# A routed two-expert layer behind linear attention: first visits of the last two routing units dispatched ahead of second ones, a third buffer of loaded rows, and one load issued two blocks earlier

## The chip, the cores and the metric

The kernel runs on one core of a Trainium2 chip. The metric is device time in microseconds (us), the median of several runs. A profiled execution gives the trace. The engines are PE (TensorE matmuls, with its weight loads PEld), DVE (VectorE), ACT (ScalarE), POOL (GpSimd) and SP (SyncE). Here POOL issues the weight loads and all indirect transfers, SP issues the other loads and stores of the routed part; all of them run on the core's 16 DMA engines.

## The reference, cut to what matters

Linear attention makes 4608 token rows of 512 values. A noisy gate picks two of eight experts for each token; each expert is a two-layer net, 512 to 1024 to 512. A token's output is the sum of its two experts' results, weighted.

```python
x = attn_out.transpose(0, 2, 1, 3).reshape(4608, 512)
logits = x @ w_gate
noisy_logits = logits + np.log1p(np.exp(x @ w_noise)) * noise
top2 = np.argpartition(-noisy_logits, 2, axis=1)[:, :2]
top2_w = softmax(noisy_logits at top2)
for e in range(8):
    for k in range(2):
        mask = top2[:, k] == e
        h = np.maximum(x[mask] @ w1[e], 0.0)
        out[mask] += top2_w[mask, k, None] * (h @ w2[e])
```

## The kernel before

**Lists.** Of a token's two experts, the one with the lower number is its first visit (kind `F`), the other its second visit (kind `S`). There are 16 lists in DRAM (`x_sorted`): one of first and one of second visits for each expert. A first visit writes its weighted result to `part`; the second visit gathers that row again (tile `L`), adds its own result and scatters the sum to the output. Tiles of kind `M` take the ends of an expert's two lists together, and their rows come by gather (tile `xm`).

**Routing.** Tokens are routed in five units (`UNITS`): units 0 to 2 have nine groups of 128 tokens each, unit 3 has six, unit 4 three. `rt_a`, `rt_b`, `rt_c` work out each token's place in its two lists (tile `posi`, written in `rt_c`). `dispatch` then sends every group twice with an indirect DMA on POOL, once for each visit (`sl` 0 and 1), and a short memset behind each keeps the issues apart. Tables of bounds (`ROUNDS`) let early loads read the front of some lists before later units have been sent; `early` declares which transfers don't touch each other's rows. Every load that has no such declaration waits until the dispatches ahead of it in the program have landed.

**Blocks.** The experts' work goes by blocks of up to 4 tiles of 128 rows. `x_load` loads a block's rows on SP: either turned by the DMA (tile `xt`), or as they are (`turned=False`, tile `xn`, from the pool `pb.np`) with the transposes done on PE in `xn_t`. `mm1` and `mm2` are the two layers, `put` stores first visits to `part` on SP and scatters second visits on POOL.

**Order.** The program is written out by hand and engines take their instructions in that order. `interval(cur, prev, weights, nxt)` interleaves three blocks on PE: the first layer of `cur`, the second layer of `prev` with its puts, and the transposes of `nxt`. The function `routing` covers the stretch that is changed; its blocks are, in order of use:

- `a0` (expert 0) and `a1` (expert 1, 3 tiles of first visits), `a2` (expert 2, 2 tiles): loaded during attention
- `b0`, `b1`, `b2` (experts 0, 1, 2; 2 tiles each) and `a3` (expert 3, 3 tiles): loaded after unit 2, by the bounds
- `c0` (expert 0, tiles 6 to 9 of first visits, 448 rows): the first block that needs its list complete, so it waits for all dispatches that can write to it

After `routing` comes a loop over `c0` and 19 more blocks. The first of the 19 (called block 1 here) is expert 1's tiles 5 and 6 of first visits; its `xn`, and the meta values of expert 1's second visits (`meta1S`), are loaded on SP behind `c0`'s load and the puts of `b2`.

In the trace the lines to know are L398 (dispatch), L442 (weights: `w1` and `w2` of an expert, 1 MB each as stored), L504 (gather of `xm`), L449 (meta loads), L571 and L574 (loads of `xn`: whole tiles, and the last half tile), L594 (PE transposes of `xn`), L647 (`mm1`), L662 (`mm2`), L630 (gather of `L`), L678 (store to `part`).

Of the kernel before, what the change touches and what calls it, by code (L numbers as in the profile page):

```python
# [7 lines left out]
FP32 = mybir.dt.float32  # L8
BF16 = mybir.dt.bfloat16
INT32 = mybir.dt.int32  # L10
# [5 lines left out]
P = 128  # L16
B, H, S, D = 8, 8, 576, 64
N_TOK = B * S
HD = H * D
E = 8  # L20
F = 1024
# [17 lines left out]
ROW_W = 576  # L39
# [81 lines left out]
class PhaseA:  # L121
# [266 lines left out]

        self.nc.gpsimd.memset(self.c["gap"], 0.0)  # L389

    def dispatch(self, u, a=0, z=9):

        tc = self.tc
        g, c0, c1 = UNITS[u]
        for ci in range(c0 + a, min(c1, c0 + z)):
            for sl in range(2):
                self.nc.gpsimd.nop()
                r = self.nc.gpsimd.indirect_dma_start(  # L398
                    out=self.x_sorted,
                    out_offset=bass.IndirectOffsetOnAxis(ap=self.r["posi", u][:, ci - c0, sl : sl + 1], axis=0),  # L400
                    in_=self.xr[g % 2][:, ci, :].bitcast(INT32), in_offset=None,
                )
                tc.declare_no_dep(r.ins, group="disp", reason="every (token, expert) pair has its own row")
                for i, (after, q) in enumerate(ROUNDS):
                    if after < u:
                        tc.declare_no_dep(r.ins, group=f"read{i}", reason="that round reads rows below its bound")
                        tc.add_to_no_dep_group(f"past{i}", r.ins)
                tc.add_to_no_dep_group("disp", r.ins)
                self.apart()


class PhaseB:
# [31 lines left out]
    def meta_load(self, e, kind, i0, nt, group=None):  # L444

        m = self.mp.tile([P, nt, 4], INT32, name=f"meta{nt}{kind}" if group is None else f"early{e}_{i0}")
        row = self.row(e, kind, i0)
        rows = self.x_sorted[row : row + nt * P, HD // 2 : HD // 2 + 4]
        r = self.nc.sync.dma_start(out=m[:], in_=rows.rearrange("(t p) c -> p t c", p=P))  # L449
        self.early(r, group)  # L450
        for i in range(nt):
            self.m[e, kind, i0 + i] = {"gate": m[:, i, 1 : 2] if kind == "F" else m[:, i, 2 : 3]}
        if kind == "S":
            self.raw[e] = m
# [90 lines left out]
        m = [P // 2 if half(*t) else P for t in tiles]  # L545
        return {"e": e, "parts": parts, "tiles": tiles, "m": m, "n": sum(m), "nt": len(m), "L": {}}

    def early(self, r, i):

        if i is not None:  # L550
            self.tc.declare_no_dep(r.ins, group=f"past{i}", reason="that round reads rows below its bound")
            self.tc.add_to_no_dep_group(f"read{i}", r.ins)

    def x_load(self, b, group=None, turned=True):


        nc, e, t = self.nc, b["e"], 0
# [5 lines left out]
        for kind, i0, n in b["parts"]:  # L563
            if kind != "M":
                row, m = self.row(e, kind, i0), sum(b["m"][t : t + n])
                src = lambda a, z: self.x_sorted[row + a : row + z, 0 : HD // 2].bitcast(BF16)
                k = m // P
                if turned:
                    r = nc.sync.dma_start(out=b["xt"][:, :, t * P : t * P + m], in_=src(0, m), transpose=True)
                else:  # L570
                    r = nc.sync.dma_start(out=b["xn"][:, t : t + k], in_=src(0, k * P).rearrange("(t p) d -> p t d", p=P))  # L571
                self.early(r, group)
                if k < n and not turned:
                    nc.sync.dma_start(out=b["xn"][0 : P // 2, t + k], in_=src(k * P, m))  # L574
            t += n

    def xn(self, b, t, dc):
# [140 lines left out]
    def general(self):  # L718

        nc, tc, c = self.nc, self.tc, self.c  # L720
# [12 lines left out]
        with tc.If(total > 0):  # L733
            for l in range(2 * E):
                e, kind = l % E, "FS"[l // E]
# [4 lines left out]
                rows = nc.values_load(ovi[0:1, l : l + 1], min_val=0, max_val=N_TOK + P)  # L740
                with tc.For_i(0, rows - (P - 1), P) as i:
                    b = self.block(e, (kind, 0, 1))
                    xn = self.mp.tile([P, ROW_W // 2], INT32, name="xn", bufs=1)
                    nc.sync.dma_start(out=xn[:], in_=self.x_sorted[bass.ds(i + l * REGION, P)])
                    tp = self.ps_y[0].tile([P, 1024], BF16, name="b")
                    for dc in range(4):
# [6 lines left out]
                    if kind == "S":  # L753
# [4 lines left out]
                        nc.vector.scalar_tensor_tensor(out=gi[:], in0=meta[:, 3:4], scalar=float(NO_P), in1=inv[:],  # L758
                                                       op0=ALU.min, op1=ALU.max)
                        nc.vector.tensor_scalar_add(out=end[:], in0=end[:], scalar1=-float(P))  # L760
                        L = b["L"][0] = self.mp.tile([P, HD], FP32, name="L", bufs=1)
                        nc.gpsimd.nop()
                        nc.gpsimd.indirect_dma_start(
                            out=L[:].bitcast(INT32), out_offset=None, in_=self.part.bitcast(INT32),
# [145 lines left out]
def routing(pa, pb, c, a0, a1, a2):  # L910
# [3 lines left out]
    a3, c0 = pb.block(3, ("F", 0, 3)), pb.block(0, ("F", 6, 4))  # L914
# [11 lines left out]
    pa.rt_c(3)  # L926
    pb.mm2(a0, 0)
    pb.put(a0, 0)
    pa.dispatch(3, 0, 3)
    pb.w_load(3, 0)  # L930
    pa.dispatch(3, 3, 6)
    pb.mm2(a0, 1)
    pb.put(a0, 1)
    pa.rt_a(4)
# [1 line left out]
    pa.rt_b(4)  # L936
    pb.mm1(a1, 6, 7)
    pa.rt_c(4)
    pa.dispatch(4)
    pb.w_load(3, 1)  # L940
    pb.mids()
    pb.meta_load(2, "F", 2, 2, 2)
    pb.x_load(b2, 2, False)
# [1 line left out]
    pb.x_load(a3, 2, False)  # L945
    pb.interval(a2, a1, (), b0)
    pb.interval(b0, a2, (), b1)
    pb.interval(b1, b0, (), b2)
    pb.interval(b2, b1, (), a3)
    pb.prepare(0)  # L950
    pb.x_load(c0, turned=False)
    pb.interval(a3, b2, (), c0)
    return a3, c0

# [19 lines left out]
def kernel(  # L974
# [24 lines left out]
    with ExitStack() as order:  # L999
        order.enter_context(tc.manual_schedule())  # L1000
        right = lambda name, bufs: ctx.enter_context(tc.tile_pool(name=name, bufs=bufs, side="right"))
        with ExitStack() as rout:
# [11 lines left out]
            pb.ps_h = [ps(ctx, "ps_h2", 3, "right")]  # L1014
            pb.ps_t = ps(ctx, "ps_t", 1, "right")
            pb.xps += [pb.xp] * 3 + [right("B_x2", 1)]
            pb.np = right("B_n", 2)
            pb.lp = right("B_l", 8)
            pb.yp += [right("B_y2", 6)] * 2
            pb.wp.append(right("B_w2", 3))  # L1020
            prev, cur = routing(pa, pb, c, *first)
        pb.ps_y.append(ps(ctx, "ps_y2", 2, "left"))
        pb.wp.append(ctx.enter_context(tc.tile_pool(name="B_w3", bufs=1, side="left")))
        blocks = [cur] + [pb.block(e, *parts) for e in range(1, E) for parts in PLAN[e]]

        todo = {}
# [55 lines left out]
```

## Time and profile before

| | us |
|---|---|
| time, median of 3 runs | 435.69 (435.42 to 435.72) |
| profiled execution, span from first to last instruction | 439.8 |
| PE matmuls busy | 353.5 (80%) |
| POOL busy | 280.4 (64%) |
| DVE busy | 185.5 (42%) |
| ACT busy | 172.9 (39%) |
| PE idle just before the transposes of `c0` | 6.4 |

The busy shares are means over the whole span: attention, with PE about half busy, takes up to some 140 us, the routed layer the rest. What a change to one stretch is worth is to be read in that stretch, from the waits and the order of the queues there. A trace time counts from the start of the span; a row of the timeline gives start, duration, engine, line, operation, tiles, count, and in brackets how long the engine was idle before it and what ended that.

### The profile page before, as it was taken

What the parts mean: (1) busy time and instruction counts of PE and PEld (TensorE: products, weight loads), DVE (VectorE), ACT (ScalarE), POOL (GpSimd) and SP (SyncE); (2) the same over time, 40 slices, a digit from 0 to 9 for tenths busy, and PEclk for the clock granted to TensorE, in tenths of its full rate; (3) what the DMA queues carried; (4) which work ended last, traced back from release to release, by engine and by line L of the source; (5) the groups of instructions that cost most, each with busy time, mean ns of one, the idle gap of its engine ahead of it and who ended that gap; (6) DMA issues with size and microseconds to landing.
All of it is one profiled execution on the core that took longest, in us unless ns stands there. A gap on an engine that the chain in (4) does not pass through costs nothing.

```text
span 439.8 us, 6877 instructions
## 1 busy us (share of the span) xinstructions
PE 353.5 (80%) x2497; PEld 211.7 (48%) x2497; DVE 185.5 (42%) x474; ACT 172.9 (39%) x310; POOL 280.4 (64%) x408
## 2 busy tenths in 40 slices
PE   3494576365745889994999999989999999999990
PEld 1293465254522456662555655644554554554440
DVE  2745989997543773120124204213331331231240
ACT  1709545760620243441444543344334334334310
POOL 7120228888888878761001848348988879778892
PEclk9858756768895699997899999999999999999996
DMA  9999997499989899999953999999988759644441
GB/s 130 206 208 207 230 213 174 107 224 236 186 192 212 165 223 213 376 211 239 233 137 109 198 211 247 215 236 194 257 177 200 212 141 232 184 150 144 154 149 51
DMA packets 83186, 85.58 MB, mean 195 GB/s; under 512 B 42656, under 2 KB 65891, under 8 KB 83143
## 3 DMA queue, kind: packets, MB, share of 16 engines
q0 software_dynamic: 36160, 63.91, 66.1%
q1 hardware_dynamic: 45318, 20.96, 21.7%
q10 hardware_dynamic: 1664, 0.18, 0.5%
q8 instruction: 21, 0.34, 0.3%
q14 instruction: 23, 0.18, 0.1%
HBM read 77.13 MB, written 33.79 MB: 252 GB/s over the span
## 4 chain that ended last, share of the span: by engine, by line
PE 45%; DMA 16%; POOL 15%; DVE 9%; issue 8%; another core or an unknown queue 2%; ACT 2%; POOLq 0%; SPq 0%; DVEq 0%; ACTq 0%
PE b L647 20%; PE b L662 20%; POOL x_sorted L398 5%; DMA v<-in_v_dram 4%; DMA w<-in_moe_w_dram 3%; DMA xn<-x_sorted 3%; POOL out_dram L684 3%; POOL L L630 3%; DMA meta5S<-x_sorted 2%; DVE xr L283 2%; DMA x_sorted<-xr,posi 1%; PE misc L209 1%; POOL gap L692 1%; DMA L<-part,gi 1%
## 5 line engine op out<-in xcount | busy, mean ns | idle before, releaser
L649 ACT ACTIVATE hT<-b 128x256 bf16<-128x256 f32 (+5 forms) x224 | 101.3, 461 | 158.0 <-PE b L647 141.4
L647 PE MATMUL b<-xt,w 128*128 128x256 bf16 (+5 forms) x896 | 153.7, 320 | 9.9 <-DMA xt<-x_sorted 4.2
L662 PE MATMUL b<-w,hT 128*128 128x512 bf16 (+1 forms) x640 | 145.8, 383 | 2.2 <-DVE y L666 2.2
L647 PEld LDWEIGHTS <-w 128*128 128x128 bf16 x896 | 88.2, 101 | 67.9 <-issue 16.2
L398 POOL DMA_INDIRECT x_sorted<-xr,posi x72 | 76.5, 1063 | 23.8 <-issue 12.2
L662 PEld LDWEIGHTS <-hT 128*128 128x128 bf16 (+1 forms) x640 | 59.3, 99 | 65.8 <-issue 6.2
L630 POOL DMA_INDIRECT L<-part,mgi x12 | 12.1, 1006 | 61.1 <-DMA part<-y 41.5
L178 ACT ACTIVATE e<-kq 128x2304 bf16<-128x2304 bf16 x16 | 33.3, 2127 | 24.4 <-DMA kq<-in_k_dram 9.4
L684 POOL DMA_INDIRECT out_dram<-y,si x34 | 33.7, 992 | 9.2 <-issue 5.1
L630 POOL DMA_INDIRECT L<-part,gi x34 | 34.9, 1027 | 6.9 <-issue 5.4
L209 PEld LDWEIGHTS <-e 64*128 64x128 bf16 x288 | 22.1, 126 | 20.0 <-DVE e L190 14.4
L272 PE MATMUL num<-kvbd,pqt 128*64 128x162 bf16 x288 | 16.8, 281 | 16.5 <-issue 9.3
L668 DVE TENSOR_SCALAR y<-b,early 128x512 f32<-128x512 f32 x18 | 13.4, 750 | 37.9 <-PE b L662 28.7
L209 PE MATMUL b<-v,e 64*128 64x192 bf16 x144 | 21.0, 320 | 10.4 <-DVE e L190 7.0
L209 PE MATMUL misc<-v,e 64*128 64x192 bf16 x144 | 20.9, 319 | 6.4 <-DMA v<-in_v_dram 6.0
L272 PEld LDWEIGHTS <-pqt 128*64 128x64 bf16 x288 | 14.0, 136 | 19.1 <-issue 10.5
L283 DVE TENSOR_TENSOR xr<-num,rden 128x768 bf16<-128x768 f32 x24 | 21.9, 952 | 0.4
L190 DVE TENSOR_TENSOR e<-e,kq 128x2304 bf16<-128x2304 bf16 x16 | 21.4, 1356 | 0.3
L637 POOL MEMSET gap<- 128x416 f32 x46 | 21.2, 462 | 0.1
L692 POOL MEMSET gap<- 128x416 f32 x45 | 20.9, 465 | 0.0
L389 POOL MEMSET gap<- 128x192 f32 x72 | 19.9, 276 | 0.0
L666 DVE SCALAR_TENSOR_TENSOR y<-b,mgate,L 128x512 f32<-128x512 f32 (+1 forms) x12 | 8.9, 746 | 25.9 <-PE b L662 10.1
(170 smaller groups left out, 314.3 us busy)
## 6 DMA issues: line engine op xcount, KB each, us to landing
w<-in_moe_w_dram POOLq DMA_DIRECT2D x16, 1024.0 KB
part<-y SPq DMA_DIRECT2D x39, 256.0 KB
kq<-in_k_dram POOLq DMA_DIRECT2D x8, 576.0 KB
kq<-in_q_dram POOLq DMA_DIRECT2D x8, 576.0 KB
v<-in_v_dram POOLq DMA_DIRECT2D x8, 576.0 KB
x_sorted<-xr,posi POOLq DMA_INDIRECT x72
xn<-x_sorted SPq DMA_DIRECT2D x4, 256.0 KB
part<-y SPq DMA_DIRECT2D x7, 128.0 KB
```

What stands on the lines that cost most here:

```text
L178: self.nc.scalar.activation(out=e, in_=x, func=ACT.Exp)
L190: nc.vector.tensor_tensor(out=e, in0=e, in1=x, op=ALU.min)
L209: nc.tensor.matmul(out=self.kvps[g, h, j][:, KVM * i : KVM * i + KVM], lhsT=e[half, hp, ci, :], rhs=v[half, hp::4, 64 * ci : 64 * ci + 64] ...
L272: nc.tensor.matmul(out=ps[half, hp, KVW * i : KVW * i + KVW], lhsT=self.pqt[g, 3 * t + i][:, hp, half], rhs=self.kvbd[g][:, j, hp, :], sta ...
L283: nc.vector.tensor_tensor(out=_ap(xr, [[64, 4], [ROW_W, 3], [1, 64]], off=3 * t * ROW_W + 256 * s), in0=_ap(ps, [[512, 4], [KVW, 3], [1, 6 ...
L398: r = self.nc.gpsimd.indirect_dma_start(out=self.x_sorted, out_offset=bass.IndirectOffsetOnAxis(ap=self.r["posi", u][:, ci - c0, sl : sl + ...
L630: r = nc.gpsimd.indirect_dma_start(out=L[0:m].bitcast(INT32), out_offset=None, in_=self.part.bitcast(INT32), in_offset=bass.IndirectOffset ...
L647: nc.tensor.matmul(out=ps[:, 0:n], lhsT=w1[:, dc, fc * P : fc * P + P], rhs=b["xt"][:, dc, 0:n], start=(dc == 0), stop=(dc == 3))
L649: nc.scalar.activation(out=b["hT"][:, fc, 0:n], in_=ps[:, 0:n], func=ACT.Relu)
L662: nc.tensor.matmul(out=ps[i * m : i * m + m], lhsT=b["hT"][:, f, t * P : t * P + m], rhs=w2[:, f, :], start=(fc == 0), stop=(fc == 8 // n ...
L684: r = nc.gpsimd.indirect_dma_start(out=self.out, out_offset=bass.IndirectOffsetOnAxis(ap=self.m[e, kind, i]["si"][0:m], axis=0), in_=y[0:m ...
L692: nc.gpsimd.memset(self.c["gap2"][:], 0.0)
```

## The change

Four things are done, all in or for the function `routing`:

- `dispatch` takes a list of visits. Unit 3 sends its six first visits, unit 4 its three, and only then do the second visits of both follow. The load of expert 3's second weight (`w_load(3, 1)`) now stands between the first and the second visits; it stood behind all dispatches.
- `early` declares that lists of first visits hold no second visits. A load from a list of first visits no longer waits for second visits, and a dispatch of second visits no longer waits for such loads. The half-tile load in `x_load` gets the same declaration.
- the pool of `xn` has three buffers, not two. To make room, two tiles of the fallback `general`, which handles overfull lists, move to a pool of their own.
- `prepare(0)` (a meta load) and `x_load(c0)` stand ahead of the intervals of `b1` and `b2`; they stood behind them.

```diff
-    def dispatch(self, u, a=0, z=9):
+    def dispatch(self, u, a=0, z=9, visits=(0, 1)):
...
-            for sl in range(2):
+            for sl in visits:
...
+                if sl:
+                    tc.declare_no_dep(r.ins, group="first", reason="lists of first visits hold no second visits")
+                    tc.add_to_no_dep_group("second", r.ins)
...
-    def early(self, r, i):
-
+    def early(self, r, kind, i):
+
+        if kind == "F":
+            self.tc.declare_no_dep(r.ins, group="second", reason="lists of first visits hold no second visits")
+            self.tc.add_to_no_dep_group("first", r.ins)
...
-                    nc.sync.dma_start(out=b["xn"][0 : P // 2, t + k], in_=src(k * P, m))
+                    r = nc.sync.dma_start(out=b["xn"][0 : P // 2, t + k], in_=src(k * P, m))
+                    self.early(r, kind, group)
...
-    pa.dispatch(3, 0, 3)
+    pa.dispatch(3, 0, 6, (0,))
     pb.w_load(3, 0)
-    pa.dispatch(3, 3, 6)
...
-    pa.dispatch(4)
+    pa.dispatch(4, visits=(0,))
     pb.w_load(3, 1)
+    pa.dispatch(3, 0, 6, (1,))
+    pa.dispatch(4, visits=(1,))
...
     pb.interval(b0, a2, (), b1)
+    pb.prepare(0)
+    pb.x_load(c0, turned=False)
     pb.interval(b1, b0, (), b2)
     pb.interval(b2, b1, (), a3)
-    pb.prepare(0)
-    pb.x_load(c0, turned=False)
     pb.interval(a3, b2, (), c0)
...
-            pb.np = right("B_n", 2)
+            pb.np = right("B_n", 3)
```

On POOL, from the load of expert 3's first weight to the first gather of `xm`, the order before is this (dispatches and their memsets repeat: six with `posi_1912`, unit 3, then six with `posi_2084`, unit 4):

```order
L442 DMA w1_1851<-in_moe_w1_dram 128x4x1024
L398 DMA x_sorted<-xr1_184,posi_1912 73984x288
...
L398 DMA x_sorted<-xr1_184,posi_2084 73984x288
...
L442 DMA w2_1852<-in_moe_w2_dram 128x8x512
L504 DMA xm_2598<-x_sorted,m_idx_2118 128x288
```

After the change three dispatches of unit 4 (`posi_2066`) come first, then the second weight, then nine dispatches of second visits (six with `posi_1912`, unit 3, and three with `posi_2066`, unit 4):

```order
L445 DMA w1_1851<-in_moe_w1_dram 128x4x1024
L398 DMA x_sorted<-xr1_184,posi_2066 73984x288
...
L445 DMA w2_1852<-in_moe_w2_dram 128x8x512
L398 DMA x_sorted<-xr1_184,posi_1912 73984x288
...
L398 DMA x_sorted<-xr1_184,posi_2066 73984x288
...
L507 DMA xm_2601<-x_sorted,m_idx_2118 128x288
```

The second weight has moved from behind twelve dispatches to behind three; the gather of `xm` still stands behind all of them.

On SP, from the last puts of `a2` (the first row) to the load of block 1 (the last row), the order before is this; the six puts between are those of `b0`, `b1` and `b2`, two each:

```order
L678 DMA part<-y_2274 128x512
L678 DMA part<-y_2323 128x512
L678 DMA part<-y_2347 128x512
L678 DMA part<-y_2407 128x512
L678 DMA part<-y_2431 128x512
L449 DMA meta4F_2475<-x_sorted 128x4x4
L571 DMA xn_2477<-x_sorted 128x3x512
L574 DMA xn_2477<-x_sorted 64x512
L678 DMA part<-y_2502 128x512
...
L449 DMA meta1S_2586<-x_sorted 128x4
L571 DMA xn_2588<-x_sorted 128x2x512
```

After the change:

```order
L685 DMA part<-y_2274 128x512
L452 DMA meta4F_2301<-x_sorted 128x4x4
L577 DMA xn_2303<-x_sorted 128x3x512
L580 DMA xn_2303<-x_sorted 64x512
L685 DMA part<-y_2328 128x512
...
L452 DMA meta1S_2589<-x_sorted 128x4
L577 DMA xn_2591<-x_sorted 128x2x512
```

The three loads for `c0` now stand ahead of the puts of `b0` and `b1`; the load of block 1 still stands behind the puts of `b2` and behind `meta1S`.

## Rows read from the trace of the kernel before

**Rows 1.** The page's part 1: busy us, share of the span, instructions.

```profile
PE 353.5 (80%) x2497; PEld 211.7 (48%) x2497; DVE 185.5 (42%) x474; ACT 172.9 (39%) x310; POOL 280.4 (64%) x408
```

**Rows 2.** Waits of PE, 140 to 440 us: who, for what: total, times, longest.

```profile
PE t L594 <- DMA xn<-x_sorted: 6.4, 1, 6.4
...
PE b L662 <- DVE y L666: 2.2, 1, 2.2
```

**Rows 3.** Timeline of PE, 184 to 300 us.

```profile
191.08 0.61 PE L594 MATMUL t<-ident,xn 128*128 128x128 bf16 x8
191.52 1.04 PE L647 MATMUL b<-xt,w 128*128 128x256 bf16 x8
...
196.91 1.46 PE L647 MATMUL b<-xt,w 128*128 128x384 bf16 x8
198.21 1.89 PE L662 MATMUL b<-w,hT 128*128 128x512 bf16 x8
206.50 1.04 PE L594 MATMUL t<-ident,xn 128*128 128x128 bf16 x8 [6.40 <-DMA xn<-x_sorted]
...
214.45 1.89 PE L662 MATMUL b<-w,hT 128*128 128x512 bf16 x8
...
219.41 0.61 PE L594 MATMUL t<-ident,xn 128*128 128x128 bf16 x8
...
295.94 1.89 PE L662 MATMUL b<-w,hT 128*128 128x512 bf16 x8 [2.16 <-DVE y L666]
```

**Rows 4.** Stretches: us, busy by engine, granted PE clock, DMA share, GB/s.

```profile
206.00:208.00 2.00, 1.50 (x11) 1.17 (x12) 0.00 (x0) 0.43 (x1) 0.00 (x0) 0.50 1.33 230
...
214.00:216.00 2.00, 2.00 (x12) 0.92 (x10) 0.00 (x0) 1.04 (x2) 0.00 (x0) 1.00 1.11 231
```

**Rows 5.** The chain that ended last, 140 to 210 us: start, us, what.

```profile
193.65 12.81 DMA xn<-x_sorted
```

**Rows 6.** Timeline of SP's queue, 100 to 302 us (the first: 178 to 181).

```profile
177.36 1.45 SPq L678 DMA_DIRECT2D part<-y  x2
...
193.65 0.82 SPq L571 DMA_DIRECT2D xn<-x_sorted  x1
...
201.80 0.48 SPq L449 DMA_DIRECT2D meta1S<-x_sorted  x1
202.38 8.83 SPq L571 DMA_DIRECT2D xn<-x_sorted  x2
...
270.28 13.57 SPq L569 DMA_TRANSPOSE xt<-x_sorted  x1
283.95 1.11 SPq L678 DMA_DIRECT2D part<-y  x2
```

**Rows 7.** Timeline of POOL, 140 to 262 us, its memsets left out.

```profile
166.23 0.82 POOL L442 DMA_DIRECT2D w<-in_moe_w_dram  x1
...
178.66 0.97 POOL L398 DMA_INDIRECT x_sorted<-xr,posi  x1 [1.58 <-DMA w<-in_moe_w_dram]
...
184.29 0.97 POOL L398 DMA_INDIRECT x_sorted<-xr,posi  x1 [0.17 <-issue]
...
189.91 1.07 POOL L504 DMA_INDIRECT xm<-x_sorted,m_idx  x1 [3.50 <-DVE y L668]
...
193.02 1.79 POOL L442 DMA_DIRECT2D w<-in_moe_w_dram  x2
```

**Rows 8.** Timeline of DVE, 150 to 240 us.

```profile
161.52 0.26 DVE L376 CAST posi<-rank 128x6 int32<-128x6 f32 x1
...
212.61 0.16 DVE L465 TENSOR_TENSOR si<-meta1S,inv 128x1 int32<-128x1 int32 x1 [11.60 <-DMA meta1S<-x_sorted]
```

**Rows 9.** Stretches of 10 us, columns as in Rows 4.

```profile
190.00:200.00 10.00, 9.77 (x66) 5.75 (x64) 1.50 (x2) 4.70 (x10) 9.36 (x12) 1.00 1.13 228
...
220.00:230.00 10.00, 10.00 (x61) 5.56 (x59) 1.87 (x3) 4.57 (x9) 0.00 (x0) 1.00 0.56 148
...
290.00:300.00 10.00, 7.84 (x40) 3.41 (x39) 3.00 (x5) 2.95 (x6) 7.81 (x11) 1.00 0.80 230
```

**Rows 10.** The last stretch, columns as in Rows 4.

```profile
396.00:440.00 44.00, 32.03 (x172) 15.69 (x170) 9.00 (x12) 10.89 (x22) 31.68 (x43) 0.90 0.38 125
```

**Rows 11.** Timeline of POOL, 345 to 400 us.

```profile
396.28 1.05 POOL L630 DMA_INDIRECT L<-part,gi  x1 [1.55 <-DMA part<-y]
```

More of the change, by code (lines that the diff above doesn't have):

```diff
@@ L449, in meta_load @@
         r = self.nc.sync.dma_start(out=m[:], in_=rows.rearrange("(t p) c -> p t c", p=P))
-        self.early(r, group)
+        self.early(r, kind, group)
         for i in range(nt):
@@ L571, in x_load @@
                     r = nc.sync.dma_start(out=b["xn"][:, t : t + k], in_=src(0, k * P).rearrange("(t p) d -> p t d", p=P))
-                self.early(r, group)
+                self.early(r, kind, group)
                 if k < n and not turned:
-                    nc.sync.dma_start(out=b["xn"][0 : P // 2, t + k], in_=src(k * P, m))
+                    r = nc.sync.dma_start(out=b["xn"][0 : P // 2, t + k], in_=src(k * P, m))
+                    self.early(r, kind, group)
             t += n
@@ L742, in general @@
                     b = self.block(e, (kind, 0, 1))
-                    xn = self.mp.tile([P, ROW_W // 2], INT32, name="xn", bufs=1)
+                    xn = self.late.tile([P, ROW_W // 2], INT32, name="xn", bufs=1)
                     nc.sync.dma_start(out=xn[:], in_=self.x_sorted[bass.ds(i + l * REGION, P)])
@@ L760, in general @@
                         nc.vector.tensor_scalar_add(out=end[:], in0=end[:], scalar1=-float(P))
-                        L = b["L"][0] = self.mp.tile([P, HD], FP32, name="L", bufs=1)
+                        L = b["L"][0] = self.late.tile([P, HD], FP32, name="L", bufs=1)
                         nc.gpsimd.nop()
@@ L1023 @@
         pb.wp.append(ctx.enter_context(tc.tile_pool(name="B_w3", bufs=1, side="left")))
+        pb.late = ctx.enter_context(tc.tile_pool(name="B_late", bufs=1, side="left"))
         blocks = [cur] + [pb.block(e, *parts) for e in range(1, E) for parts in PLAN[e]]
```

## The prediction, made before the changed kernel ran

> **What bounds the kernel now.** I read the busy times first: PE is the busiest engine, 353.5 of 439.8 us [rows 1]. So what counts behind the attention part is PE's own waits. From 140 us to the end PE waits for a transfer once: 6.4 us in its transposes (L594) for a load of `xn`; the next one is 2.2 us for DVE, at 294 us [rows 2]. PE's timeline places the first: PE has ended its work at 200.10 and stands until 206.50 [rows 3]. The chain of waits names the load: issued on SP at 193.65, landed 12.81 later, at 206.46 [rows 5]; by the order on SP this is the load of `c0`. The idle stretch has a second price. In the stretch 206 to 208 us the granted clock is 0.50, that is 1.2 of 2.4 GHz, and at 214 to 216 us it is 1.00 again [rows 4]; ahead of the wait it was 1.00 [rows 9]. Between the two, PE works at half speed.
>
> From there to the end PE stands close to its work: its only larger gap is the 2.16 us at 294 us [rows 3]. The last stretch belongs to POOL, which gathers and scatters expert 7's tiles one behind the other from 396.28 on (31.68 us busy in the stretch, PE 32.03) [rows 10]; but that row of tiles starts when a store to `part` has landed [rows 11], a store of a result of PE. So a time that PE gains at 200 us is passed on to the end unless something between is bound by transfers.
>
> **The change part by part.**
>
> *The load of `c0` moves up.* Now it stands on SP behind the puts of `b1`, and reaches the queue at 193.65 [rows 6]. After the change it stands behind the last put of `a2`. SP ends that put at 178.81 [rows 6]. The load then needs the nine first visits of units 3 and 4. Unit 4's places are worked out at 161.8 [rows 8], so its first visits can be sent right behind the weight load of 166.23, in the places that unit 3's dispatches had. POOL has eight transfers in flight: the one at 178.66 stood 1.58 us for the weight load eight places before it, so this one landed at about 178.5 [rows 7], and I take the three dispatches behind it to land by 180. So `c0`'s load is issued at about 181, not 193.65. With the duration it had, 12.81 [rows 5], it lands at about 194, six us ahead of 200.10. It lands no sooner than the dispatches, so 181 is the floor; the ceiling is the first rival. The wait of 6.40 us goes.
>
> *The half clock goes with it.* From 206.50 to 214.45 PE ran 8 transposes, 8 matmuls of 384 columns, 8 transposes and 16 matmuls of 384 columns [rows 3]: 7.95 us. At full clock 8 transposes took 0.44 (191.08 to 191.52) and 8 such matmuls 1.30 (196.91 to 198.21) [rows 3]. Full speed makes 0.44 + 1.30 + 0.44 + 2.60 = 4.78. Saved: 3.17 us. Together 6.40 + 3.17 = **9.57 us**.
>
> *What is late next.* Block 1's transposes stand at 219.41 now, without a wait [rows 3]; with 9.57 less they stand at 209.84. Its load doesn't move: it is issued at 202.38, behind `meta1S` and the puts of `b2`, which still follow PE [rows 6]. Its 256 KB may take 12.81 x 256/448 = 7.3 us if the duration goes by size (landed at 209.7, no wait), or 12.81 if it goes by what else is under way (215.2, wait 5.35). `meta1S`, issued at 201.80, landed by 212.61, 10.8 us later, with `c0`'s load ahead of it [rows 6, 8]; without that it will be quicker. I take the middle of the two bounds, 10.0 us: landed at 212.4, a wait of **2.5 us**, since the two weight loads issued at 193.02 [rows 7] will be under way then as they were beside `c0`'s load. Such a wait keeps the clock: after the 2.16 us at 294 us it is 1.00 over the whole stretch [rows 3, 9].
>
> Here a page speaks for less. The Trainium skill ("DMA: Bandwidth & Descriptors", section on the anatomy of one DMA) fits a DMA from GpSimd with 2.0 us plus bytes over 436 GB/s, which would be 2.9 us for the 384 KB of `c0`'s larger load and, an estimate by that page, 2.6 us for block 1's; then the wait of 2.5 falls away and the sum is 430.2. The trace disagrees for a queue under load: 12.81 us.
>
> *The third buffer.* With two, SP stood inside the two loads issued from 202.38 for 8.83 us [rows 6], until `c0`'s transposes had freed a buffer. With three it goes on at once. Nothing that PE waits for stands behind it there, so I cost it at nothing; without it `c0`'s early load would have to wait for the transposes of `b2`, which is why it belongs to the first item.
>
> *First visits first, and the weight between.* The number of dispatches, memsets and weight loads on POOL is the same. What moves is the weight's 1 MB: from behind the last dispatch to ahead of nine. Its first use is the second layer of `a3`, now at 214.45 [rows 3], then about 205; it is earlier in both. The second visits land later by what the weight takes, at most 166.23 to 178.5, 12.3 us [rows 7], and by what `c0`'s load takes of the DMA engines. Who waits: the gather of `xm` at 189.91 [rows 7], all of POOL behind it (four weight loads for experts 4 and 5) and `meta1S` on SP. PE needs `xm` only for the block behind block 1 and the weights far behind, and the DMA engines, full at 190 to 200 us (share 1.13), are half idle at 220 to 230 (0.56) [rows 9]; so this is covered as long as the second visits have landed when SP comes to `meta1S` at 201.80. I expect them at 195 to 199: 189.91 and 5 to 9 us. The puts of `b0` and `b1` come behind `c0`'s load on SP; their results wait in buffers and nobody on PE waits for the stores.
>
> *Behind 220 us.* The 2.16 us at 294 us come from a gather that waited for a store, which stood on SP behind a load (270.28, 13.57 us) [rows 6] that waits for PE to free its buffer. That goes with PE, so I leave it as it is.
>
> The sum against the profiled span: 439.8 - 9.57 + 2.5 = 432.7. The median of the runs stands to that span as 435.69 to 439.8, 0.9907: **428.7 us**.
>
> **The rivals.**
>
> 1. *`c0` is late still.* Its load meets the weight that was moved up. If the weight's 12.3 us come wholly ahead of it, it lands at 181 + 12.3 + 12.81 = 206.1, and all but 0.4 us stays: 435.3. If half of it, at 200.0, and nothing stays. Against it: the two are in different queues and the load's own 12.81 was measured beside two weight loads. 0.05.
>
> 2. *Block 1 takes the place of `c0`.* Its load takes the full 12.81, PE stands 5.35 us and the clock halves again, 3.17: 439.8 - 9.57 + 5.35 + 3.17 = 438.75, so 434.7. For it: a wait of 6.40 did that to the clock, one of 2.16 didn't. Without the clock it is 431.5, the upper end of my forecast. 0.05.
>
> 3. *Behind 220 us the transfers set the time.* Then the gather behind the 294 us wait comes when it came before and the gain is waited away: 435.7. Against it: DMA shares of 0.56 ahead of that stretch [rows 9], and PE's results as what the stores wait for. 0.04.
>
> 4. *Slower: SP stands at `meta1S`.* It waits for all second visits, and block 1's load, of first visits, stands behind it. If weight and `c0`'s load both come wholly ahead of the second visits, these have landed not at 189.9 but at 189.9 + 12.3 + 12.81 = 215.0; block 1's load then lands 10.0 later at 225.6 with its issue, PE stands 15.8 us and the clock halves: 439.8 - 9.57 + 15.8 + 3.17 = 449.2, so 445.0. It decides from 206 on: there the wait and the half clock eat the 9.57. The DMA engines are full from 190 us on, which speaks for it; that neither transfer has the engines for itself during its whole time speaks against. 0.06.
>
> The rule beside this one is in the Trainium skill ("Trainium Kernel Development and Optimization", Key Constraints): DMAs from SP, ACT and POOL all run on the same 16 engines and interleave. By it a load that is moved up takes its share from the others, and the shares above 1 agree.
>
> **How the numbers follow.** The forecast, 0.80, has its own range from no wait at block 1 and some tenths of luck beyond (430.2 by the span, 426.2; I take 425.8) to a wait of 5.35 at full clock (431.5). This holds 8 in 10, so it is the range: 425.8 to 431.6. A measurement of this kernel tells 0.2%, 0.87 us, from no change. Faster by more: 0.80 and some 0.07 of rivals 1 and 2; slower: rival 4, 0.06; the rest, 0.07, within.
>
> **What would show it.** Right: no idle time of PE before the transposes of `c0`, clock 1.00 from 190 to 220 us; `c0`'s load issued on SP at about 181; a wait of 0 to 5 us at block 1's transposes, for `xn`; the gather of `xm` at 195 to 200; the 2 us wait for DVE some 7 us earlier. Wrong: PE waiting at `c0` still, SP standing at `meta1S` past 206, or the wait near 294 us longer by what was gained.

## The result and the profile after

The changed kernel takes **429.57 us** (427.49 to 432.09, 4 runs) where the kernel before takes 435.71 (435.42 to 435.94): ratio 0.9846, interval 0.9802 to 0.989. That lies 0.9 us above the forecast of 428.7 and inside its range. The profiled execution has a span of 427.3 us. In the whole document a median is over all executions, and a ratio leaves out those that took over 1.5% longer than the fastest of their kernel.

In the code of after, L398 is still the dispatch; L445 is the weight load, L507 the gather of `xm`, L577 and L580 the loads of `xn`, L601 the transposes of `xn`, L654 and L669 the two layers, L673 and L675 the DVE operations that read a result of the second layer, L637 the gather of `L`, L685 the store to `part`.

The waits of PE from 140 to 430 us in after (who, for what: total, times, longest):

```profile
PE b L669 <- DVE y L675: 5.2, 1, 5.2
PE b L654 <- DMA xt<-x_sorted: 2.2, 1, 2.2
```

The 6.4 us for `xn` of [rows 2] are gone, and so are the 2.2 us for DVE. A new wait of 5.2 us has come. PE's timeline in after (start, duration, engine, line, operation; in brackets the idle time before it and what ended it):

```profile
192.25 0.61 PE L601 MATMUL t<-ident,xn 128*128 128x128 bf16 x8
...
202.33 0.61 PE L601 MATMUL t<-ident,xn 128*128 128x128 bf16 x8
...
256.38 3.57 PE L669 MATMUL b<-w,hT 128*128 128x512 bf16 x8 [5.17 <-DVE y L675]
```

The first row is `c0`, where [rows 3] has 6.40 us of idle time; the second is block 1. Neither waits, and both run at full speed: 0.61 us for 8 transposes, as in [rows 3] ahead of the wait. The third row stands in the second layer of block 4: 8 matmuls that take 1.89 us at full clock take 3.57. The stretches (us, busy by engine, granted clock, DMA share, GB/s) show the clock and the load on the DMA engines:

```profile
190.00:194.00 4.00, 4.00 (x29) 2.30 (x27) 1.05 (x3) 2.08 (x4) 0.00 (x0) 1.00 0.58 217
...
220.00:230.00 10.00, 9.95 (x69) 6.41 (x69) 2.13 (x9) 4.54 (x11) 3.84 (x5) 1.00 1.27 204
...
256.00:262.00 6.00, 5.62 (x26) 2.68 (x27) 3.06 (x5) 1.20 (x4) 5.23 (x8) 0.56 1.03 178
```

Against [rows 9] the picture is turned round: the engines have a gap at 190 us (0.58), and at 220 to 230 us they are full (1.27, before 0.56). The queues say why. First SP, then POOL without its memsets, both in after:

```profile
178.16 0.76 SPq L577 DMA_DIRECT2D xn<-x_sorted  x1
180.98 1.86 SPq L580 DMA_DIRECT2D xn<-x_sorted  x1
...
194.36 0.33 SPq L452 DMA_DIRECT2D meta1S<-x_sorted  x1
194.79 0.89 SPq L577 DMA_DIRECT2D xn<-x_sorted  x2
```

```profile
168.10 0.96 POOL L445 DMA_DIRECT2D w<-in_moe_w_dram  x1
...
186.61 0.96 POOL L398 DMA_INDIRECT x_sorted<-xr,posi  x1 [6.11 <-DMA w<-in_moe_w_dram]
...
194.30 1.05 POOL L507 DMA_INDIRECT xm<-x_sorted,m_idx  x1 [5.05 <-DMA x_sorted<-xr,posi]
...
197.38 1.80 POOL L445 DMA_DIRECT2D w<-in_moe_w_dram  x2
...
202.65 1.78 POOL L445 DMA_DIRECT2D w<-in_moe_w_dram  x2
```

`c0`'s load is issued at 178.16, 15.5 us sooner than in [rows 6]. On POOL the weight that was moved up (168.10) holds back the last second visits by 6.11 us: the transfer issued at 186.61 is the eighth behind that weight and goes when it has landed (186.3). The gather of `xm` waits 5.05 us more, and the four weight loads of experts 4 and 5 go from 197.38 on, not from 193.02 [rows 7]; counted from the common mark of the next paragraph that is 11.9 us later. The first of them stands 5.1 us behind PE's start on `c0` (192.25); before, it stood 13.5 us ahead of it (206.50).

One stretch makes the executions comparable, since they differ by several us already in attention. ACT writes `hT` 224 times. From the end of the 49th write (about 180 us) to the end of the 145th (about 300) lies what the change is seen to move on PE: from there to the 224th and last write it takes 108.47 us in before and after alike, and what follows that write 15.8 us in before and 15.2 in after. Within the stretch four pieces of eight writes each hold the waits:

| kernel, its profile | stretch | `c0` | block 1 | block 5 | block 8 |
|---|---|---|---|---|---|
| before | 128.67 | 19.22 | 11.19 | 10.48 | 12.85 |
| before, again | 130.35 | 18.94 | 11.20 | 10.47 | 14.85 |
| after | 124.39 | 9.81 | 11.20 | 18.06 | 10.53 |
| after, again | 124.76 | 9.80 | 11.21 | 18.42 | 10.53 |
| after, third | 123.37 | 9.81 | 13.15 | 10.52 | 14.46 |

(The pieces run from the end of the 57th, 65th, 105th and 129th write over eight each; the first two are named for the block whose transposes stand in them, the others for the block whose first layer does. The wait near 256 us, in the second layer of block 4, falls into the piece of block 5, and that of 294 us [rows 3] into block 8's. "After, third" comes from the last experiment.) In the first pair the change takes 9.41 us out of the first piece, gives 7.58 back in the third, and 2.32 go from the fourth: 4.15 of the stretch's 4.28.

### The profile page after: what moved, and what is told of

Same layout as the page of the kernel before. It is cut to its first block, busy times and chain, and to the rows that moved or that the text cites. A ratio compares the mean times of both kernels' runs of the same rounds, so it can differ in the third digit from the quotient of the medians.

```text
span 427.3 us, 6850 instructions
## 1 busy us (share of the span) xinstructions
PE 350.8 (82%) x2467; PEld 211.3 (49%) x2497; DVE 184.5 (43%) x474; ACT 173.0 (40%) x310; POOL 279.5 (65%) x408
## 4 chain that ended last, share of the span: by engine, by line
PE 46%; POOL 23%; DMA 14%; DVE 6%; issue 6%; ACT 2%; POOLq 0%; SPq 0%; DVEq 0%
PE b L669 21%; PE b L654 20%; POOL x_sorted L398 10%; DMA L<-part,mgi 4%; DMA v<-in_v_dram 4%; POOL L L637 3%; POOL gap L389 3%; POOL out_dram L691 3%; DMA x_sorted<-xr,posi 3%; DMA part<-y 2%; PE misc L209 1%; POOL gap L644 1%; PE b L209 1%; DVE e L190 1%; POOL gap L699 1%
## 5 line engine op out<-in xcount | busy, mean ns | idle before, releaser
L654 PE MATMUL b<-xt,w 128*128 128x256 bf16 (+5 forms) x892 | 149.5, 314 | 12.5 <-DMA xt<-x_sorted 9.7
L669 PE MATMUL b<-w,hT 128*128 128x512 bf16 (+1 forms) x614 | 146.5, 388 | 7.1 <-DVE y L675 5.2
L654 PEld LDWEIGHTS <-w 128*128 128x128 bf16 x896 | 86.5, 99 | 68.0 <-issue 16.4
L669 PEld LDWEIGHTS <-hT 128*128 128x128 bf16 (+1 forms) x640 | 59.9, 100 | 70.9 <-issue 12.3
L398 POOL DMA_INDIRECT x_sorted<-xr,posi x72 | 74.9, 1040 | 29.1 <-issue 11.9
L178 ACT ACTIVATE e<-kq 128x2304 bf16<-128x2304 bf16 x16 | 33.3, 2127 | 23.6 <-PE misc L209 12.1
L637 POOL DMA_INDIRECT L<-part,gi x34 | 34.8, 1024 | 7.9 <-issue 6.3
L637 POOL DMA_INDIRECT L<-part,mgi x12 | 12.1, 1005 | 40.0 <-DMA part<-y 22.9
L675 DVE TENSOR_SCALAR y<-b,early 128x512 f32<-128x512 f32 x18 | 13.4, 749 | 34.5 <-PE b L669 30.6
L272 PE MATMUL num<-kvbd,pqt 128*64 128x162 bf16 x288 | 17.7, 292 | 10.8 <-DVE lwt L290 10.1
L673 DVE SCALAR_TENSOR_TENSOR y<-b,mgate,L 128x512 f32<-128x512 f32 (+1 forms) x12 | 8.9, 745 | 32.3 <-DMA L<-part,mgi 18.8
L389 POOL MEMSET gap<- 128x192 f32 x72 | 21.0, 292 | 0.0
## 6 DMA issues: line engine op xcount, KB each, us to landing
kq<-in_q_dram POOLq DMA_DIRECT2D x8, 576.0 KB, 14.7
```

Of the source, the lines that this page charges most:

```text
L178: self.nc.scalar.activation(out=e, in_=x, func=ACT.Exp)
L272: nc.tensor.matmul(out=ps[half, hp, KVW * i : KVW * i + KVW], lhsT=self.pqt[g, 3 * t + i][:, hp, half], rhs=self.kvbd[g][:, j, hp, :], sta ...
L398: r = self.nc.gpsimd.indirect_dma_start(out=self.x_sorted, out_offset=bass.IndirectOffsetOnAxis(ap=self.r["posi", u][:, ci - c0, sl : sl + ...
L637: r = nc.gpsimd.indirect_dma_start(out=L[0:m].bitcast(INT32), out_offset=None, in_=self.part.bitcast(INT32), in_offset=bass.IndirectOffset ...
L654: nc.tensor.matmul(out=ps[:, 0:n], lhsT=w1[:, dc, fc * P : fc * P + P], rhs=b["xt"][:, dc, 0:n], start=(dc == 0), stop=(dc == 3))
L669: nc.tensor.matmul(out=ps[i * m : i * m + m], lhsT=b["hT"][:, f, t * P : t * P + m], rhs=w2[:, f, :], start=(fc == 0), stop=(fc == 8 // n ...
```

## The experiments

**Both kernels again.** The same two kernels once more, beside the next two experiments.

> The kernel before, profiled once more. Theory (the gain is the wait at c0 and the half clock behind it): PE again waits some 6 us for xn ahead of the transposes of c0, with the clock at 0.50 behind it; time 435.7, span about 434. The 8.74 us in which PE stood at 126 to 136 us in the first profile was of that execution alone. Rival (the wait at c0 is an accident of the first profile): no wait over 2 us at c0, and the changed kernel's 6 us come from elsewhere.

> The changed kernel once more. Theory: no wait at c0; the wait of PE for DVE before the second layer of block 3 (5.17 us at 251 us in its first profile) is there again, with a size that goes with the landing of the gathers of L ahead of it; time 428 to 431, with a spread of some 4 us. Rival (that wait was an accident of one execution): no wait over 2 us behind c0, and time 427.5, the lowest seen.

Before: 438.31 us (435.18 to 440.75; a second series of the same kernel beside it 437.02). After: 431.42 (430.13 to 433.04), ratio 0.9886 (0.983 to 0.9942). The profiles repeat the first ones: before waits 6.97 us at `c0`, after waits 5.47 us near 256 us. (This is the wait that the second expectation puts before block 3's second layer, at 251 us: it begins at 251.2, and the matmuls behind it are of block 4.)

**The second weight of expert 3 behind the second visits.**

```diff
-    pb.w_load(3, 1)
     pa.dispatch(3, 0, 6, (1,))
     pa.dispatch(4, visits=(1,))
+    pb.w_load(3, 1)
```

> Undoes one part: the second weight of expert 3 stands behind the second visits again. Theory (the weight between the visits delays the second visits, the gather of xm and all weights behind it): POOL stands no 6 us in its dispatches, xm is gathered some 5 us earlier, the weights of experts 4 and 5 end some 5 us earlier, the gathers of L for block 2 land in 4 to 7 us instead of 7 to 12, and PE's wait near 251 us is 0 to 3 us: 425 to 428. Rival 1 (the same bytes move, so nothing is won): 429.6 within 1. Rival 2 (the second layer of a3 comes to wait for the weight, needed at 197.4): slower than 430.

432.4 us (429.56 to 433.45), ratio 0.9896 (0.9838 to 0.9954): as after beside it (431.42). But the wait is another one, which none of the three expectations foresaw. PE's timeline there has one wait between 185 and 262 us:

```profile
206.03 1.04 PE L601 MATMUL t<-ident,xn 128*128 128x128 bf16 x8 [3.95 <-DMA xn<-x_sorted]
```

It is block 1, with half clock (1.04 for 0.61). POOL doesn't stand for the weight now, the four weights go from 190.93 on, and block 1's load, issued at 195.40, takes 10.6 us; in after it was issued at 194.79 and took 3.2. `c0`'s load, issued at 177.29 with no weight under way until 181.70, takes 7.5 us, not 12.9 as in after. In return the weights end sooner (224.7, not 229.3), and nothing waits near 256 us. So the weight moved up is a trade: it spares block 1 and charges block 4.

**The weights of experts 5 to 7 one or two blocks later.**

```diff
-WEIGHTS = [(0, 0), (1, 1), (2, 3), (4, 5)]
+WEIGHTS = [(0, 0), (2, 3), (4, 5), (6, 7)]
```

> The changed kernel, with the weights of experts 5, 6 and 7 issued one to two blocks later each (expert 5's behind the gathers of L for block 2). Theory (expert 5's weights are what these gathers and the stores ahead of them lie under): the gathers land in 3 to 5 us, no wait of PE near 251 us: 5.2 us and some 2.5 of half clock less: 422 to 425. Rival 1 (the turned loads on SP's queue are what the gathers lie under): the wait stays, 429 to 431. Rival 2 (the weights now come too late for experts 5 to 7): a wait for w in the first layer of those blocks, 430 or more.

> The weights of experts 5, 6 and 7 later, once more, to see what its slower executions (430 to 435, beside 423 to 425) have that its first profile lacks. Theory (a wait that comes and goes with the landing of transfers): this profile, if it is of a slower execution, has a wait of PE of 4 us or more at c0, block 1 or block 4 that the first had not. Rival (the spread is of the attention part, as in the kernel before): the routed part from 150 us on takes the same time as in the first profile within 1 us.

The same kernel twice: 431.31 us (423.01 to 435.1) and 432.26 (424.84 to 435.77). Its executions spread over 12 us, so its time can't be told from after's. Its two profiles, of executions of 424.7 and 424.8 us, agree: three pieces at full speed (9.81, 11.20, 10.47), 11.58 and 11.42 in the fourth, stretches of 117.86 and 117.69, and behind 180 us the first has only one wait of PE for a transfer or for DVE, the second two, of 1.6 us together (waits of PE, first profile):

```profile
PE b L669 <- DVE y L673: 0.9, 1, 0.9
```

With two 1 MB loads fewer in POOL's queue the gathers of `L` for block 2 take 4.0 to 4.8 us (second profile), not 6.9 to 12.0, and the wait near 256 us is gone. So the profiled executions fit the first theory, wait and time, and the medians don't. Why the other executions are longer, no profile shows: both are of short ones.

**`c0`'s load back behind the puts of `b1`.** The order of visits, the declarations and the third buffer stay.

```diff
-    pb.prepare(0)
-    pb.x_load(c0, turned=False)
     pb.interval(b1, b0, (), b2)
     pb.interval(b2, b1, (), a3)
+    pb.prepare(0)
+    pb.x_load(c0, turned=False)
```

> Undoes one part: c0's meta and row loads stand behind the puts of b1 again; dispatch order, declarations and third buffer stay. Theory (the early issue of this load is the gain): it is issued at about 191, PE comes to c0 at about 192, stands 4 to 8 us for xn and works at half clock behind it; 434 to 438. Rival (the order of the visits alone gives the gain, since the load no longer waits for second visits): no wait over 2 us, 430 to 432.

430.93 us (426.58 to 431.52), ratio 0.9899 (0.9827 to 0.997). The theory that the early place of the load removes the wait falls. SP's queue, then PE's timeline:

```profile
187.08 0.39 SPq L577 DMA_DIRECT2D xn<-x_sorted  x1
```

```profile
193.79 0.62 PE L601 MATMUL t<-ident,xn 128*128 128x128 bf16 x8 [0.19 <-DMA xn<-x_sorted]
```

The load is issued 8.9 us later than in after and lands at 193.8, not 191.1: it takes 6.7 us, not 12.9, while no weight is under way (one landed at 185.4, the next is issued at 196.51). PE waits 0.19 us. Counted from the 49th write of `hT`, the load is issued at 6.6 us, in before at 6.8: its place is that of before, and only what is under way beside it differs.

**Visits alternate again.** The early load, the declarations and the third buffer stay; dispatches and weights stand as before.

```diff
-    pa.dispatch(3, 0, 6, (0,))
+    pa.dispatch(3, 0, 3)
     pb.w_load(3, 0)
+    pa.dispatch(3, 3, 6)
...
-    pa.dispatch(4, visits=(0,))
+    pa.dispatch(4)
     pb.w_load(3, 1)
-    pa.dispatch(3, 0, 6, (1,))
-    pa.dispatch(4, visits=(1,))
```

> Undoes one part: first and second visits of units 3 and 4 alternate again, expert 3's second weight behind them; the early load, its declarations and the third buffer stay. Theory (the load needs the last first visit, which now lands at about 186): SP stands at c0's meta load until then, the rows land near 199, PE waits 4 to 6 us at c0 at half clock behind it: 433 to 437. Rival (the place of the load on SP is enough): the load lands before 192, no wait at c0, 429 to 432.

436.94 us (433.74 to 442.95), ratio 1.004 (0.9987 to 1.0093): the gain is gone. The time lies in the range of the theory, but the wait stands elsewhere. PE's timeline:

```profile
195.30 0.62 PE L601 MATMUL t<-ident,xn 128*128 128x128 bf16 x8 [1.60 <-DMA xn<-x_sorted]
...
211.17 1.03 PE L601 MATMUL t<-ident,xn 128*128 128x128 bf16 x8 [5.63 <-DMA xn<-x_sorted]
```

`c0` waits only 1.60 us, but the weights go from 188.06 on, and block 1's load, issued at 198.43, takes 12.7 us: PE waits 5.63 us for it and then runs at half clock. Pieces 11.58 and 18.91, stretch 130.17, as long as before's (128.67 and 130.35). With the experiment ahead of it this says which part of the change does the work: the new order on POOL (first visits first, with the weight between and the declarations) gives the gain without the early load; the early load without that order shrinks the wait at `c0` and puts another at block 1. Order of visits and place of the weight weren't tried apart from each other with the load in its old place.

**Two buffers.**

```diff
-            pb.np = right("B_n", 3)
+            pb.np = right("B_n", 2)
```

> Undoes one part: two buffers of xn. Theory now: b2's transposes are over at 176.2 in the changed kernel's trace and c0's load is issued at 178.2, so its buffer is free and nothing is lost; 430 to 432, no wait at c0. Rival (the step of the prediction that gave the third buffer a part in the early load): the load is held up, PE waits at c0; 433 or more.

426.89 us (425.85 to 429.83), ratio 0.9854 (0.9786 to 0.9921), below both expectations. No wait comes back at `c0` or block 1 (9.81, 11.20). SP's queue:

```profile
177.90 0.85 SPq L577 DMA_DIRECT2D xn<-x_sorted  x1
...
204.26 0.37 SPq L577 DMA_DIRECT2D xn<-x_sorted  x1
```

`c0`'s load goes as early as with three; what the third buffer moves is the load of block 2, issued at 204.26 here and at 196.76 in after, and PE waits for neither. Near 256 us PE waits 1.93 us here. That this kernel is faster than after isn't settled, since the intervals of the two overlap and after's own profiles have that wait at 5.2, 5.5 and 0 us.

**All later weights two blocks later or more,** in the kernel before, in after, and in after with two buffers; and after once more.

```diff
-WEIGHTS = [(0, 0), (1, 1), (2, 3), (4, 5)]
+WEIGHTS = [(2, 3), (4, 5), (6, 7), (8, 9)]
```

> The changed kernel again, beside the three others of this call. Both theories: 427.5 to 431.5 us, the 5 us wait of PE for DVE near 256 us there in its profile, as in the last look (5.5 us).

> The kernel before, with the weight loads of experts 4 to 7 issued two blocks later or more (WEIGHTS from (0, 0), (1, 1), (2, 3), (4, 5) to (2, 3), (4, 5), (6, 7), (8, 9)); visits alternate, c0's load stands where it stood. Theory W (what makes the loads of x rows long is a weight load of 1 MB in flight on POOL's queue, and the order of visits works by holding weights back): c0's load still meets the second half of expert 3, which landed at 196.0 in the last look at the kernel before, but no other: a wait of 0.5 to 4 us at c0 in place of 7.0, none at block 1, no half clock or less of it: 428 to 433 us. Theory D (c0 needs its load issued early, or the first visits to come first): the wait of 6 to 7 us and the half clock stay: 434.5 to 437.5.

> The changed kernel with the same later weights, so that none is in flight from 186 to 228 us. Theory W: the wait at the block of expert 4 (5.2 to 5.5 us, with 2.5 us of half clock) goes, since store and gathers no longer share with weights: 7 to 8 us less than the changed kernel of this call, 421 to 425. Rival (that wait comes from POOL's and SP's order, not from the weights): no more than 2 us less, 427 to 431. A second rival: the weights, two blocks later, meet the transposing loads at 255 to 275 us, and PE waits there for 2 us or more: 425 to 428.

> The same with two buffers of loaded rows in place of three. If the third buffer does nothing for PE (its load of block 2 is 6 us earlier, and no one waits): within 1 us of the kernel with late weights and three buffers. If the early load of c0 needs it: a wait for xn of 2 us or more comes back between 190 and 215 us.

(The wait that one of these texts puts at the block of expert 4 is the one near 256 us, in block 4, which is of expert 2.) After: 435.09 us (430.66 to 440.0; before, beside it, 441.14, 434.49 to 453.18), ratio 0.9854 (0.974 to 0.9968). The others are slower than before: 457.44, ratio 1.0437 (1.0364 to 1.0511); 450.56, 1.0255 (1.0162 to 1.0348); 455.08, 1.0209 (1.0082 to 1.0336). So the times fall outside every expectation (after's too, with before 4 to 6 us above its other medians), while the stretch does what the first theory said, and more: no wait at `c0`, where it left 0.5 to 4 us.

| kernel | stretch | `c0` | block 1 | block 5 | from there to the last write |
|---|---|---|---|---|---|
| before, weights late | 121.10 | 9.81 | 11.20 | 10.46 | 123.17 |
| after, weights late | 119.70 | 9.81 | 11.20 | 10.47 | 124.07 |
| after, weights late, two buffers | 119.54 | 9.80 | 11.20 | 10.47 | 120.28 |

In the kernel before, which keeps its order of visits and its late load, the whole wait at `c0` is gone with the later weights, 9.25 us of the stretch against the 130.35 of before's second profile. But expert 3's second weight was out of the way too in this execution: it landed at 199.5, as the load was issued (199.59). In that second profile it landed at 196.1, and so was under way for 6.1 of the load's 13.3 us. Here the load took 5.7 us and landed 0.6 us before PE came. So the run shows that `c0` doesn't wait when no weight is under way beside its load; the share of the four weights isn't separated from that of expert 3's. The loss lies behind the stretch: 14.7 us more than the usual 108.47 to the last write, and 5.9 more behind that. Waits of PE behind 300 us in that kernel's timeline:

```profile
325.41 0.61 PE L612 MATMUL t<-ident,xm 128*128 128x128 bf16 x4 [4.53 <-DMA xm<-x_sorted,m_idx]
...
334.29 1.89 PE L662 MATMUL b<-w,hT 128*128 128x512 bf16 x8 [1.95 <-DVE y L666]
```

Expert 7's weights now go at 308.01 and 326.97 and take 23.2 and 23.6 us, and the gather of `xm` stands in the same queue. I moved four experts' weights where two weight loads were in question; the experiment answers for the stretch and not for a better kernel. The third profile of after has no wait near 256 us but one at block 1:

```profile
209.06 0.62 PE L601 MATMUL t<-ident,xn 128*128 128x128 bf16 x8 [1.77 <-DMA xn<-x_sorted]
```

**What all of them show together** is the time of a load of rows on SP against the weight loads on POOL. Block 1's 256 KB:

| kernel | load issued | next weight issued behind expert 3's | load takes |
|---|---|---|---|
| after; again; two buffers; expert 5 later | 194.79; 195.43; 196.08; 196.10 | 197.38; 197.22; 198.22; 197.56 | 3.2; 2.9; 3.2; 3.3 |
| weights late, in before; in after | 208.33; 200.98 | 241.09; 233.63 | 2.9; 2.9 |
| load of `c0` back; after, third | 196.99; 199.59 | 196.51; 198.63 | 7.2; 9.4 |
| expert 3's weight last; visits alternate; before | 195.40; 198.43; 202.38 | 190.93; 188.06; 193.02 | 10.6; 12.7; 13.6 |

(With the weights of expert 5 later, two weights follow there and not four.) Issued 1.5 us or more ahead of the first weight the load takes 3 us, 0.5 to 1.0 behind it 7 to 9, 4.5 us or more behind it 10.6 to 13.6. Whether block 1 waits in after is a race of SP against POOL that is won by 1.8 to 2.6 us, and in one profile lost by 1.0.

## Why the prediction was right, and where not

*The wait at `c0` and its half clock, 9.57 us.* Right in size and place: 9.41 in the first profiles, 9.14 in the second pair. The load was issued at 178.16 (predicted about 181) and took 12.91 us (12.81), so it landed at 191.07, before the predicted 194. But the early issue, which the prediction gives as the reason, isn't needed: the wait goes also with the load in its old place, and with later weights. What counts is whether `c0`'s load meets one of the four weights: in the three profiles in which it does (before twice, alternating visits) PE waits 1.6 to 7.0 us, in all others 0.4 us at most. Without the new order on POOL the early issue left 1.60 us of the wait. With it, the load meets expert 3's weight instead: counted from the end of the 49th write, it is issued 7.7 us sooner than with the load back, and lands 1.5 us sooner. That it took as long as in before, where other weights were beside it too, is luck.

*Block 1's wait, 2.5 us.* Measured: 0, 0 and 1.8 us. The step that failed is "the two weight loads issued at 193.02 will be under way then as they were beside `c0`'s load". The same text lets the gather of `xm` wait until 195 to 200, "all of POOL behind it"; the weights are behind it, so they couldn't be under way from 193 on. The two statements were not put together. The 2.6 us that the Trainium skill ("DMA: Bandwidth & Descriptors", the anatomy of one DMA) gives for this load, an estimate by that page (its fit is for a DMA from GpSimd, this load is SP's), is close to the 2.9 to 3.3 us measured where no weight is under way; beside weights the runs disagree, with 7.2 to 13.6 us. Rival 2, that block 1 takes the place of `c0`, is what the alternating visits with the early load did: 5.63 us and half a clock, 436.94 us where 434.7 was worked out.

*"So this is covered."* This step failed, and at 7.6 us it cost more than the missing wait at block 1 (2.5) and the fourth piece (2.3) gave back. The text counted the half idle DMA engines at 220 to 230 us as room for what comes later. The weights did go there and ended at 229.3 us (223.4 before). But what follows PE came there as well: block 2's gathers are issued from 225.83 on, not from 240.04, and expert 6's weights behind them. Here is the chain of waits of after (start, us, what):

```profile
229.21 12.00 DMA L<-part,mgi
...
242.84 1.17 DMA part<-y
```

and DVE's timeline of after:

```profile
232.81 0.75 DVE L673 SCALAR_TENSOR_TENSOR y<-b,mgate,L 128x512 f32<-128x512 f32 x1 [8.17 <-DMA L<-part,mgi]
...
255.32 0.16 DVE L523 TENSOR_TENSOR msi<-xm,m_gone 128x2 int32<-128x2 int32 x1 [7.48 <-DMA out_dram<-y,msi]
...
255.58 1.41 DVE L675 TENSOR_SCALAR y<-b,meta2F 128x512 f32<-128x512 f32 x2
```

DVE rewrites `msi`, the indices that block 2's scatter reads, and must wait until that scatter has landed. The scatter stands in POOL's queue behind two weight loads of expert 6, which landed at 246.1 and 254.0; POOL's timeline:

```profile
230.56 0.84 POOL L445 DMA_DIRECT2D w<-in_moe_w_dram  x1
...
234.78 0.97 POOL L445 DMA_DIRECT2D w<-in_moe_w_dram  x1
236.05 1.05 POOL L691 DMA_INDIRECT out_dram<-y,msi  x1 [0.30 <-issue]
```

It lands at 254.3, the last of its kind at 255.3. Behind this on DVE stand the reads of block 3's results (255.58), and for these PE waits. In before the order on POOL is the same and DVE stood there as well, but it was released before PE needed it (timeline of DVE, the kernel before):

```profile
266.61 0.16 DVE L520 TENSOR_TENSOR msi<-xm,m_gone 128x2 int32<-128x2 int32 x1 [7.75 <-DMA out_dram<-y,msi]
```

Counted from the end of the 105th write of `hT`, DVE is released after 3.5 us in before, 9.3 in after, 7.4 with `c0`'s load back, 6.0 with two buffers, 4.0 in the third profile of after, 2.5 with expert 5's weights later. PE's waits are 0, 5.17, 3.34, 1.93, 0 and 0: always what exceeds 4.1 us. In after the gathers go 20.2 us ahead of that mark and take 6.9 to 12.0 us; in before they go 23.1 ahead and take about 4. So what rival 3 says, that transfers behind 220 us set the time, held for 7.6 of the 9.4 us, though at 256 us and not at 294. The prediction had it as all or nothing, and a loss in part had no place in its sum.

*The wait of 2.16 us at 294 us "goes with PE".* In after's first two profiles it is gone, behind a loss of 7.6 and 7.9 us near 256; in the third, without that loss, it is back with 2.08 us. Where the wait near 256 us is smaller, both stand: 3.34 and 2.31 with `c0`'s load back, 1.93 and 1.78 with two buffers. That the first takes the second away is argued, not shown.

*Second visits, 195 to 199, and the gather of `xm`, 195 to 200.* The last second visit landed at 193.4, and the gather went at 194.30: both a little sooner. `meta1S` was no stand for SP (194.36, then the next load at once), so rival 4 stayed away. Weight and `c0`'s load shared the engines, as the Trainium skill ("Trainium Kernel Development and Optimization", Key Constraints) has it for DMAs of different queues: the load took 12.91 us beside that weight, 6.67 without.

*The third buffer,* said to be what lets `c0`'s load go early: wrong, with two buffers it goes as early. The transposes of `b2`, for which it was to wait, begin at 175.77 in after and take 0.61 us.

So the total came out close, 429.57 for 428.7, by terms that differ: 9.4 for 9.57 gained, 0 for 2.5 lost at block 1, 7.6 lost near 256 us and 2.3 gained at 294 us that the sum didn't have: 4.1 us of the stretch in the first profiles and 5.6 in the second pair, with 7.07 predicted. With the 0.6 us behind the stretch that is 4.9 and 6.2 us by the profiles, where the medians differ by 6.1 and 6.9; the rest isn't placed. That the total came so near is luck in part: the terms that the sum lacked, 7.6 us of loss against 2.5 and 2.3, happened to leave a small difference. The two profiled spans differ by more, 12.5 us, but 7.5 of these lie ahead of the stretch, which starts at 186.8 and 179.3 and is mostly preceded by attention, where the code is the same: the end of the 49th write lies between 178.9 and 192.9 us over all profiles.

## What to carry to other kernels

The load that PE waited for here was short or long by what the other queue sent at that moment, so ask of a reordering first which large transfers it delays, and only then which load it brings forward. Idle transfer time later in the profile wasn't room for what was pushed there: PE got earlier, and its next gathers and stores arrived in that place too. And a row in which an engine waits for a transfer without holding up PE, as DVE did for the scatter of block 2, should be noted with its slack (4.1 us less 3.5 here), since a gain upstream uses it up.

## What the runs showed of the hardware

Block 1's load of 256 KB took between 2.9 and 13.6 us, by what 1 MB loads of another queue were under way. Transfers of POOL's queue landed in the order of their issue, as far as the traces tell their landing: a scatter behind two weight loads took 18.3 us.

The half clock doesn't follow from the length of a wait. After 3.34 us (load of `c0` back) 8 matmuls took 1.89 us, full clock; after 2.08 us (third profile of after) they took 3.42. The wait of 2.16 us of [rows 3], at full clock behind it, came again in the second profile of before with 2.47 us, and there the 8 matmuls took 3.03. PE's timelines of the first two:

```profile
256.49 1.89 PE L669 MATMUL b<-w,hT 128*128 128x512 bf16 x8 [3.34 <-DVE y L675]
```

```profile
285.60 3.42 PE L669 MATMUL b<-w,hT 128*128 128x512 bf16 x8 [2.08 <-DVE y L673]
```

The prediction's "such a wait keeps the clock" was drawn from one row and doesn't hold in general. What decides it stays open, and so does the spread of whole executions: the medians of the kernel before were 435.7, 437.0, 435.4 and 441.1 us beside the four groups of runs, and in the profiles the part ahead of the stretch varies most. Two series of it beside each other differ by 0.3% (437.02 and 438.31), so the 0.2% by which the prediction would tell a change was too fine.
